# One-pass attention ahead of two gated layers: the first two pairs interleaved, casts moved from ScalarE to VectorE, squares issued earlier, two banks instead of one

## The chip, the cores and the metric
One core of one Trainium2 chip runs the whole program. The metric is device time in microseconds (us). Three runs of the kernel before gave 581.31, 584.41 and 585.79 us, median 584.41 us. The execution that the profiler recorded took 581.65 us; its span, from the first to the last recorded instruction, is 579.8 us.

## The reference, cut to what matters
Inputs are `q`, `k`, `v` of shape (2, 12, 448, 64) in fp32 and a scalar `cap`.

```python
scores = cap * np.tanh((q @ k.T / sqrt(64)) / cap)
attn   = softmax(scores)                 # exp, divided by (row sum + 1e-09)
x      = (attn @ v) laid out as (896 tokens, 768 features)
xn     = x / sqrt(mean(x * x) + 1e-06) * rms_g
y      = (silu-gated product of xn @ w_gate and xn @ w_val) @ w_out
out    = prelu(y @ w_in, alpha) @ w_out2
```

The change touches only the first part, from the scores to `xn`, and the weight preparation that runs beside it.

## The kernel before
**Pairs.** The 24 heads are handled as 12 pairs of heads (`NPAIR`), one pair per turn of the main attention loop; "step i" below is turn i. A pair's 2 x 448 x 448 scores are seven 128-row tiles, worked on as four groups: groups 0, 1 and 2 hold two tiles each (128 x 896), group 3 (`TG`) holds one tile with the last 64 keys of both heads. A group's scores are three products (`qk`, L204: high with high parts, low with high, high with low), because each fp32 operand is split into a rounded part `hi` and a rest `lo`. "Score group (i, g)" below is group g of pair i.

**PSUM.** Groups 0 and 1 take turns in two slots of two banks (`ps_s`, tag "s"). Groups 3 and 2 share one further slot (`third()`, tag "x"), one after the other: the second must wait until ScalarE has read the first. One slot `upper()` (tag "o") holds the value product of a pair (`pv`, L231), one slot tag "u" the row sums (`sums`, L245) or a normalisation factor (`under()`).

**A step.** The order is written out by hand; no scheduler moves it, and every engine executes its part strictly in the order of the program text. In step i TensorE (PE) makes the scores of pair i, then the row sums and the value product of pair i-1. ScalarE (ACT) applies tanh to each score group and one exp to the whole pair (`soft`, L213 and L218). VectorE (DVE) copies the value product of pair i-2 out of PSUM (`evac_o`, tile `ee`, L270), takes reciprocals of row sums that come back by DMA (`recip`, L290 to L301), splits the operands of pair i+1 into `hi` and `lo` (`prep`, L187, L188), and copies the row sums out (`evac_u`, L278) and sends them by DMA (L281).

**Every second step.** For even i from 4 on, two finished pairs are normalised (`norm`, L328, L329): PE spreads the reciprocals over 128 partitions (tile `rps`), DVE multiplies. The first of these products of PE goes to slot "u", the second to slot "o", so the second can only start after DVE's copy `ee` has emptied "o". GpSimd (POOL) then squares the normalised pairs (`square`, L308 to L316), and in step 9 PE adds the squares of the first batch up (`rms_sum`, tile `ms`, L350), which is followed by a square root on ACT in step 9 and a reciprocal on DVE in step 10.

**Weights beside it.** Eight units of packed first-layer weights (`conv[0]` to `conv[7]`, 128 x 768 each) are unpacked meanwhile, one per step: `w_top` (L112, a cast of every fourth bf16 into every second f16, on ACT), `w_bits` (L117, DVE), and for some `w_hi` (L131, a cast, on ACT) and `w_lo` (L136, DVE). POOL forms sums and differences of whole units (`w_sum`, L125; named `sum1` to `sum4`, for two halves g = 0 and 1). The lists `first` and `second` hold these side jobs: `a(i, job)` issues one after the softmax of step i, `z(i, job)` at the end of step i.

Of the kernel before, what the change touches and what calls it, by code (L numbers as in the profile page):

```python
# [7 lines left out]
F32 = mybir.dt.float32  # L8
# [49 lines left out]
def attn_moe_kernel(ctx: ExitStack, tc: tile.TileContext, units, qk_in, v, sel, w, gvec, alpha, cap, out, out_t):  # L58
# [46 lines left out]

    top_of = {}

    def w_top(u):
        n = width(u)
        top_of[u] = tops[n_top[0] % 2][:, :n]  # L110
        n_top[0] += 1
        nc.scalar.copy(top_of[u].bitcast(F16)[:, 1::2], raw_t[u].bitcast(BF16)[:, 4:4 * n + 4:4])  # L112

    def w_bits(u):
        n = width(u)
# [9 lines left out]
        nc.gpsimd.tensor_tensor(out=t, in0=f_t[a], in1=f_t[b], op=op)  # L125
        f_t[out] = t

    def w_hi(u):
        k = width(u) // P if u in units else UK
        h_t[u] = wpool.tile([P, UK, P], F32R, tag="wh", name="wh", bufs=WH)[:, :k]  # L130
        nc.scalar.copy(h_t[u], f_t[u].rearrange("p (k m) -> p k m", m=P))  # L131

    def w_lo(u):
        k = width(u) // P if u in units else UK
# [60 lines left out]
    def third():  # L195
        return ps_x.tile([P, 2, 512], F32, tag="x", name="s")
# [11 lines left out]
    def soft(i):  # L208
        t = pt[i] = sb.tile([P, TILES, S], F32, tag="pt", name="pt")
        done = 0  # L210
        for g in (TG, *range(TG)):
            w = WIDE[g]
            nc.scalar.activation(  # L213
                out=t[:, 2 * g:2 * g + w], in_=st.pop((i, g))[:, :w, :S], func=AF.Tanh, scale=cinv
            )
            if g == TG - 1 or (i == 0 and g == 1):
                to = TILES if g == TG - 1 else 4
                nc.scalar.activation(out=t[:, done:to], in_=t[:, done:to], func=AF.Exp, scale=cap_t)  # L218
                done = to

# [2 lines left out]
    def upper(name):  # L223
        return ps_o.tile([P, 512], F32, tag="o", name=name)

    def pv(i):
        t, vv = pt[i], vt.pop(i)
        oo[i] = upper("oo")
        for c in range(TG + 1):
            for h in range(2):  # L230
                nc.tensor.matmul(  # L231
                    oo[i][h * D:h * D + D, :S], vv[:, 2 * c + h, :], t[:, min(2 * c + h, TILES - 1), :], start=c == 0,
                    stop=c == TG, skip_group_check=True,
                )
        del hi[i], lo[i]

    def tiles_of(i):
        return [pt[i][:, min(n, TILES - 1)] for n in range(TILES + 1)]
# [86 lines left out]
    def norm(i, rps):  # L325
        b, p = divmod(i, NP)
        n, j = group[i]
        nc.tensor.matmul(rps[:, :S], sel_t[:, j, :], r2[n % 2], start=True, stop=True)  # L328
        nc.vector.tensor_tensor(out=xf[b][:, p, :], in0=ee.pop(i), in1=rps[:, :S], op=ALU.mult)  # L329
# [90 lines left out]
    with tc.manual_schedule():  # L420
# [41 lines left out]
        def a(i, fn, *args):  # L462
            first.setdefault(i, []).append((fn, args))

        def z(i, fn, *args):
            second.setdefault(i, []).append((fn, args))
# [5 lines left out]
        for i in range(NPAIR):  # L472
            if i % 2 == 1 and i > 2:
                a(i, recip, (i - 3) // 2)
            a(i, load_raw, i + 2)
            a(i, load_v, i + 1)
            a(i, prep, i + 1)
            if i - 2 in range(len(conv)):
                a(i, w_bits, conv[i - 2])
                if i - 2 < len(conv) - RAW:  # L480
                    a(i, w_next, conv[i - 2])
            if i - 1 in range(len(conv)):
                a(i, w_top, conv[i - 1])
            if i % 2 == 0 and i > 2:
                for j in range(2):
                    z(i, square, i - 4 + j)
        a(9, rms_root, 0)
        for hi_at, lo_at, j in ((3, 4, 0), (4, 5, 1), (9, 10, 6), (11, None, 7)):
            a(hi_at, w_hi, conv[j])
            if lo_at:  # L490
                a(lo_at, w_lo, conv[j])
        for put, n, fn, g in ((z, 6, sum1, 0), (z, 7, sum1, 1), (z, 7, sum2, 0), (a, 8, sum2, 1), (a, 8, sum3, 0),
                              (z, 8, sum3, 1), (z, 10, sum4, 0)):
            put(n, fn, "g", g)
# [3 lines left out]
        for i in range(NPAIR):  # L498
            pairs = i % 2 == 0 and i > 2
            if i > 1:  # L500
                evac_o(i - 2)
            if pairs:
                norm(i - 4, under())
            qk(i, TG, third())
            if pairs:
                norm(i - 3, upper("rps"))
            if i == 9:
                rms_sum(0, upper("ms"))
                rms_keep(0)
                nc.vector.tensor_copy(rstd[0], ms_of[0][:, :S])  # L510
                ms_of[0] = rstd[0]
            for g in range(TG):
                qk(i, g, third() if g == TG - 1 else ps_s.tile([P, 2, 512], F32, tag="s", name="s"))
            soft(i)
            for fn, args in first.pop(i, []):
                fn(*args)
            if i == 1:
                pv(0)
            if i > 0:
                sums(i - 1)  # L520
                evac_u(i - 1)
            if i > 1:
                pv(i - 1)
            if i > 0:
                del pt[i - 1]
            for fn, args in second.pop(i, []):
                fn(*args)
        assert not first and not second
        evac_o(last - 1)
        x = third()  # L530
        for j in range(2):
            norm(last - 3 + j, x[:, j])
        sums_now(last)
        pv(last)
        xnorm(2)
# [633 lines left out]
```

## Time and profile before

| | |
|---|---|
| runs | 581.31, 584.41, 585.79 us |
| profiled execution | 581.65 us, span 579.8 us |
| PE busy | 566.8 us (98% of the span) |
| DVE busy | 393.8 us (68%) |
| ACT busy | 340.1 us (59%) |
| POOL busy | 110.2 us (19%) |
| chain that ended last | PE 87%, DVE 4%, POOL 3%, ACT 2%, issue 2% |

An engine's share over the whole span says little here, since the attention steps fill about the first 112 us and the layers the rest. The places where PE stands still are what the table does not show; they are in the rows further down. Times in the rows are from the start of the span. A row of the timeline that merges several instructions gives the time from the first to the last of them.

### The profile page before, as it was taken

Reading aid. Unit: us, or ns where it says so; the run is one execution under the profiler, and the core shown is the slowest. Engines: PE = TensorE matmul, PEld = TensorE weight load, DVE = VectorE, ACT = ScalarE, POOL = GpSimd, SP = SyncE. Lnnn points to the kernel's source line nnn. Section 1 sums busy time; section 2 is a strip of 40 time slices with the busy share of each in tenths; the row PEclk is TensorE's granted clock in tenths of the full one; section 3 lists DMA queues with packets and bytes.
Section 4 is the critical chain, followed back from the end, with each engine's and each line's share of the span. In section 5 each row is a group of like instructions: output and inputs, shape, how many; then the busy total and the mean of one; then the engine's idle time right before and its main releaser. Section 6 shows DMA issues by size and latency. Waiting matters only on the chain.

```text
span 579.8 us, 7286 instructions
## 1 busy us (share of the span) xinstructions
PE 566.8 (98%) x2891; PEld 469.7 (81%) x2891; DVE 393.8 (68%) x445; ACT 340.1 (59%) x398; POOL 110.2 (19%) x60
## 2 busy tenths in 40 slices
PE   7999988999999999999999999999999999999997
PEld 5544434389899999999999999999999988888996
DVE  5377778799998796769761644979897987522400
ACT  6999979557645644448543443595687877323301
POOL 0022564110044342310000054401451000000000
PEclk9999999999999999999999999999999999999999
DMA  8455511120136335124541653003421335343201
GB/s 274 161 197 181 171 57 44 47 119 1 55 109 218 110 109 167 51 63 155 199 137 46 224 212 110 0 1 118 154 74 37 110 109 181 99 164 126 103 0 64
DMA packets 17946, 66.05 MB, mean 114 GB/s; under 512 B 3704, under 2 KB 4344, under 8 KB 17912
## 3 DMA queue, kind: packets, MB, share of 16 engines
q1 hardware_dynamic: 17336, 65.07, 33.3%
q8 instruction: 23, 0.38, 0.3%
q10 hardware_dynamic: 432, 0.38, 0.2%
q0 software_dynamic: 144, 0.13, 0.1%
q14 instruction: 11, 0.09, 0.0%
HBM read 62.66 MB, written 2.75 MB: 113 GB/s over the span
## 4 chain that ended last, share of the span: by engine, by line
PE 87%; DVE 4%; POOL 3%; ACT 2%; issue 2%; DMA 0%; SPq 0%; POOLq 0%
PE s L401 22%; PE m L401 18%; PE m L690 10%; PE s L714 8%; PE m L714 6%; PE s L690 5%; PE s L740 5%; PE s L204 3%; PE oo L231 3%; PE m L740 2%; POOL wt L125 1%; PE us L245 1%; PE m L414 1%; PE s L414 1%; ACT pt L213 1%
## 5 line engine op out<-in xcount | busy, mean ns | idle before, releaser
L136 DVE TENSOR_TENSOR wl<-wt,wh 128x768 fp32r<-128x768 f32 (+2 forms) x104 | 111.2, 1074 | 79.6 <-ACT wh L131 78.5
L125 POOL TENSOR_TENSOR wt<-wt 128x768 f32<-128x768 f32 x40 | 89.2, 2238 | 262.5 <-DVE wt L117 151.2
L131 ACT CAST wh<-wt 128x768 fp32r<-128x768 f32 (+2 forms) x104 | 82.3, 796 | 90.0 <-PE m L714 24.0
L401 PE MATMUL s<-xx,wh 128*128 128x448 f32 x420 | 100.6, 366 | 0.1
L112 ACT CAST top<-raw 128x768 f16<-128x768 bf16 (+2 forms) x74 | 73.8, 1005 | 41.9 <-DVE wt L117 33.8
L401 PEld LDWEIGHTS s<-xx,wh 128*128 128x128 f32 x420 | 78.7, 188 | 7.7 <-issue 0.9
L117 DVE SCALAR_TENSOR_TENSOR wt<-raw,top 128x768 uint32<-128x768 uint32 (+2 forms) x74 | 72.2, 978 | 0.0
L401 PE MATMUL m<-xx,wh 128*128 128x448 f32 x252 | 60.3, 365 | 0.0
L401 PE MATMUL s<-xx,wl 128*128 128x448 f32 x210 | 54.0, 365 | 0.0
L401 PEld LDWEIGHTS m<-xx,wh 128*128 128x128 f32 x252 | 47.3, 188 | 3.7
L213 ACT ACTIVATE pt<-s,cinv 128x896 f32<-128x896 f32 (+1 forms) x48 | 41.3, 913 | 10.0 <-PE s L204 9.4
L401 PEld LDWEIGHTS s<-xx,wl 128*128 128x128 f32 x210 | 39.4, 188 | 3.1
L231 PE MATMUL oo<-pt,vt 128*64 128x448 f32 x192 | 38.7, 545 | 0.0
L218 ACT ACTIVATE pt<-pt,cap_t 128x3136 f32<-128x3136 f32 (+2 forms) x13 | 35.2, 2711 | 0.4
L231 PEld LDWEIGHTS oo<-pt,vt 128*64 128x64 f32 x192 | 12.8, 136 | 24.8 <-issue 19.0
L401 PE MATMUL m<-xx,wl 128*128 128x448 f32 x126 | 32.3, 365 | 0.0
L690 PE MATMUL m<-b,wh 128*128 128x448 f32 x96 | 27.3, 365 | 0.0
L204 PE MATMUL s<-hi 64*128 64x448 f32 (+1 forms) x84 | 21.5, 440 | 5.0 <-ACT pt L213 4.8
L714 PE MATMUL s<-wh,xx 128*128 128x512 f32 x72 | 25.4, 389 | 0.0
L401 PEld LDWEIGHTS m<-xx,wl 128*128 128x128 f32 x126 | 23.7, 188 | 1.9
L690 PE MATMUL m<-xx,wl 128*128 128x448 f32 x88 | 25.0, 365 | 0.0
L690 PE MATMUL m<-xx,wh 128*128 128x448 f32 x88 | 25.0, 365 | 0.0
(210 smaller groups left out, 1004.3 us busy)
## 6 DMA issues: line engine op xcount, KB each, us to landing
raw<-w_in SPq DMA_DIRECT2D x57, 768.0 KB
raw<-w_in SPq DMA_DIRECT2D x16, 512.0 KB
rw<-qk_in SPq DMA_DIRECT2D x11, 480.0 KB
vt<-v_in SPq DMA_DIRECT2D x12, 256.0 KB
out<-wt SPq DMA_DIRECT2D x7, 256.0 KB
out<-o SPq DMA_DIRECT2D x1, 448.0 KB
gt<-us SPq DMA_DIRECT2D x22, 3.5 KB
rw<-qk_in ACTq DMA_DIRECT2D x1, 256.0 KB
```

Of the source, the lines that this page charges most:

```text
L112: nc.scalar.copy(top_of[u].bitcast(F16)[:, 1::2], raw_t[u].bitcast(BF16)[:, 4:4 * n + 4:4])
L117: nc.vector.scalar_tensor_tensor(out=f_t[u].bitcast(U32), in0=raw_t.pop(u).bitcast(U32)[:, 1:2 * n + 1:2], scalar=13, in1=top_of.pop(u), o ...
L125: nc.gpsimd.tensor_tensor(out=t, in0=f_t[a], in1=f_t[b], op=op)
L131: nc.scalar.copy(h_t[u], f_t[u].rearrange("p (k m) -> p k m", m=P))
L136: nc.vector.tensor_tensor(out=l_t[u], in0=f_t[u].rearrange("p (k m) -> p k m", m=P), in1=h_t[u], op=ALU.subtract)
L204: nc.tensor.matmul(s[:, h, :S], kt[rows, c:c + P], qt[rows, :S], start=m == 0, stop=m == 2, skip_group_check=True,)
L213: nc.scalar.activation(out=t[:, 2 * g:2 * g + w], in_=st.pop((i, g))[:, :w, :S], func=AF.Tanh, scale=cinv)
L231: nc.tensor.matmul(oo[i][h * D:h * D + D, :S], vv[:, 2 * c + h, :], t[:, min(2 * c + h, TILES - 1), :], start=c == 0, stop=c == TG, skip_g ...
L401: nc.tensor.matmul(ps[:, r, :S], lhs, rhs, start=first and n == 0, stop=n == len(mm) - 1, skip_group_check=True,)
L690: nc.tensor.matmul(dst[l], wt[:, o, :], x[l], start=first and wt is wh and x is xh, stop=stop)
L714: nc.tensor.matmul(banks[t // 2][:, t % 2], x[:, c], wt, start=j == 0 and n == 0, stop=j == K2N - 1 and n == 2,)
L740: nc.tensor.matmul(dst[m, l], wt[:, o, :], x[:, l], start=k == 0 and n == 0, stop=k == K2N - 1 and n == 2,)
```

## The change
Five things are edited; what is computed stays the same.

1. **First two pairs.** Step 0 makes its groups in the order 0, 1, 2, 3 instead of 3, 0, 1, 2, and group 3 of pair 0 moves from the slot `third()` to a slot of `ps_s`. The tanh calls of pair 0 follow the same order. In step 1 the value product of pair 0 is cut in two halves, one after score group (1, 0), one after (1, 1), where it stood after all four groups.
2. **Casts to DVE.** `w_top` of the first four units goes from ACT to DVE, to the end of steps 1 to 4. `w_hi` of units 0, 1 and 6 goes from ACT to DVE, to the end of steps 3, 4 and 9, with `w_lo` right behind it (it stood in the steps after).
3. **Squares ahead.** In step 8 the squares of pairs 4 and 5 are issued before two of the weight sums on POOL.
4. **Row sums ahead.** In step 10 the row sums of pair 9 are made before score group (10, 2).
5. **Banks apart.** The last two normalisations after the loop use two different slots; they were halves of one.

```diff
-    def w_top(u):
+    def w_top(u, copy=nc.scalar.copy):
...
-        nc.scalar.copy(top_of[u].bitcast(F16)[:, 1::2], raw_t[u].bitcast(BF16)[:, 4:4 * n + 4:4])
+        copy(top_of[u].bitcast(F16)[:, 1::2], raw_t[u].bitcast(BF16)[:, 4:4 * n + 4:4])
...
-        for g in (TG, *range(TG)):
+        for g in (*range(TG), TG) if i == 0 else (TG, *range(TG)):
...
-    def pv(i):
-        t, vv = pt[i], vt.pop(i)
-        oo[i] = upper("oo")
-        for c in range(TG + 1):
+    def pv(i, cs=range(TG + 1)):
+        t, vv = pt[i], vt[i]
+        if cs[0] == 0:
+            oo[i] = upper("oo")
+        for c in cs:
...
-            if i - 1 in range(len(conv)):
-                a(i, w_top, conv[i - 1])
             if i % 2 == 0 and i > 2:
                 for j in range(2):
-                    z(i, square, i - 4 + j)
+                    (a if i == 8 else z)(i, square, i - 4 + j)
+            if i - 1 in range(len(conv)):
+                if i < 5:
+                    z(i, w_top, conv[i - 1], nc.vector.tensor_copy)
+                else:
+                    a(i, w_top, conv[i - 1])
         a(9, rms_root, 0)
-        for hi_at, lo_at, j in ((3, 4, 0), (4, 5, 1), (9, 10, 6), (11, None, 7)):
-            a(hi_at, w_hi, conv[j])
-            if lo_at:
-                a(lo_at, w_lo, conv[j])
+        for n, j in ((3, 0), (4, 1), (9, 6)):
+            z(n, w_hi, conv[j], nc.vector.tensor_copy)
+            z(n, w_lo, conv[j])
+        a(11, w_hi, conv[7])
...
-            qk(i, TG, third())
+            if i:
+                qk(i, TG, third())
...
-            for g in range(TG):
-                qk(i, g, third() if g == TG - 1 else ps_s.tile([P, 2, 512], F32, tag="s", name="s"))
+            two = lambda: ps_s.tile([P, 2, 512], F32, tag="s", name="s")
+            for g in range(TG - 1):
+                qk(i, g, two())
+                if (i, g) == (1, 0):
+                    pv(0, range(2))
+            if i == 0:
+                qk(0, TG - 1, third())
+                qk(0, TG, two())
+            if i == 1:
+                pv(0, range(2, TG + 1))
+            if i == 10:
+                sums(i - 1)
+            if i:
+                qk(i, TG - 1, third())
...
-        x = third()
-        for j in range(2):
-            norm(last - 3 + j, x[:, j])
+        norm(last - 3, third()[:, 0])
+        norm(last - 2, under())
```

What this makes of the order, at three places. First TensorE in step 1 (`s` a score group, `oo` the value product of pair 0, `us` its row sums); ahead of this piece stand the score groups (1, 3) and (1, 0), and before the change also (1, 1) and (1, 2):

```order
-L231 MATMUL oo<-pt,vt 64x448 x8
+L232 MATMUL oo<-pt,vt 64x448 x4
+L204 MATMUL s<-hi 128x448 x2
+L204 MATMUL s<-hi,lo 128x448 x2
+L204 MATMUL s<-lo,hi 128x448 x2
+L232 MATMUL oo<-pt,vt 64x448 x4
+L204 MATMUL s<-hi 128x448 x2
+L204 MATMUL s<-hi,lo 128x448 x2
+L204 MATMUL s<-lo,hi 128x448 x2
 L245 MATMUL us<-pt,ones 32x448 x6
```

The value product of pair 0 now stands in two halves around score group (1, 1), and score group (1, 2) has gone behind both.

Second, VectorE at the end of step 3 and in step 4 (`us` the copied row sums, `top`, `wh`, `wl` the weight jobs, `ee` the copy that empties slot "o"):

```order
 L117 SCALAR_TENSOR_TENSOR wt<-raw,top_94 128x768
 L278 COPY us<-us 128x448
+L112 CAST top_93<-raw 128x768
+L131 CAST wh<-wt 128x768
+L136 TENSOR_TENSOR wl<-wt,wh 128x768
 L270 COPY ee<-oo 128x448
 L329 TENSOR_TENSOR xf<-ee,rps 128x448 x2
```

Three weight jobs now stand ahead of the copy `ee` of pair 2; in step 9 two of them (`wh`, `wl`) stand in the same way ahead of the copy of pair 8.

Third, GpSimd from step 6 to step 8 (`wt` weight sums, `sq` squares, `s` their running sum, whose number is only a name):

```order
-L316 TENSOR_TENSOR s_473<-s_473,sq 128x448
-L125 TENSOR_TENSOR wt<-wt 128x768 x5
+L316 TENSOR_TENSOR s_470<-s_470,sq 128x448
+L125 TENSOR_TENSOR wt<-wt 128x768 x3
 L312 TENSOR_TENSOR sq<-xf 128x448
-L316 TENSOR_TENSOR s_473<-s_473,sq 128x448
+L316 TENSOR_TENSOR s_470<-s_470,sq 128x448
 L312 TENSOR_TENSOR sq<-xf 128x448
-L125 TENSOR_TENSOR wt<-wt 128x768
+L125 TENSOR_TENSOR wt<-wt 128x768 x3
```

Two weight sums have moved from in front of the squares of pairs 4 and 5 to behind them.

## Rows read from the trace of the kernel before

**Rows 1.** Windows, attention and a later stretch: stretch, length, engines' busy us, PEclk, DMA share, GB/s.

```profile
0.00:116.00 116.00, 106.96 (x673) 53.52 (x674) 78.76 (x117) 95.58 (x86) 35.10 (x27) 0.99 0.43 142
116.00:200.00 84.00, 83.68 (x406) 75.74 (x405) 78.03 (x86) 49.85 (x66) 19.12 (x9) 1.00 0.28 97
```

**Rows 2.** Waits of PE, 0 to 122 us: total us, times, longest us.

```profile
PE s L204 <- ACT pt L213: 4.8, 2, 2.9
PE ms L350 <- POOL s L316: 1.7, 1, 1.7
...
PE s L328 <- DVE xf L329: 0.9, 1, 0.9
PE rps L328 <- DVE us L278: 0.4, 1, 0.4
```

**Rows 3.** Windows of one us around PE's first long wait; columns as in rows 1.

```profile
13.00:14.00 1.00, 1.00 (x3) 0.72 (x3) 0.00 (x0) 1.00 (x1) 0.00 (x0) 0.50 1.02 424
...
17.00:18.00 1.00, 1.00 (x8) 0.34 (x6) 0.00 (x0) 1.00 (x2) 0.00 (x0) 1.00 0.58 224
```

**Rows 4.** Timeline of PE, steps 1 to 3: start us, us, what, idle before.

```profile
12.93 0.70 PE L204 MATMUL s<-hi 128*128 128x448 f32 x1 [2.93 <-ACT pt L213]
...
17.30 3.23 PE L231 MATMUL oo<-pt,vt 128*64 128x448 f32 x16
20.45 1.32 PE L245 MATMUL us<-pt,ones 128*32 128x448 f32 x10
...
22.09 0.47 PE L204 MATMUL s<-hi 128*128 128x448 f32 x1
...
29.74 0.47 PE L204 MATMUL s<-hi 128*128 128x448 f32 x1
```

**Rows 5.** ACT: first tanh in the timeline.

```profile
6.62 0.63 ACT L213 ACTIVATE pt<-s,cinv 128x448 f32<-128x448 f32 x1 [0.24 <-PE s L204]
```

**Rows 6.** Lines of ACT by shape, 0 to 112 us: count, busy us, mean ns, idle before.

```profile
L213 ACT ACTIVATE pt<-s,cinv 128x896 f32<-128x896 f32 x36 | 33.9, 1006 | 7.1 <-PE s L204 6.8
L218 ACT ACTIVATE pt<-pt,cap_t 128x3136 f32<-128x3136 f32 x11 | 32.0, 2913 | 0.4
L112 ACT CAST top<-raw 128x768 f16<-128x768 bf16 x8 | 8.5, 1056 | 0.0
L213 ACT ACTIVATE pt<-s,cinv 128x448 f32<-128x448 f32 x12 | 7.6, 634 | 3.0 <-PE s L204 2.5
L131 ACT CAST wh<-wt 128x768 fp32r<-128x768 f32 x4 | 3.3, 818 | 0.0
L218 ACT ACTIVATE pt<-pt,cap_t 128x1792 f32<-128x1792 f32 x1 | 1.8, 1788 | 0.0
```

**Rows 7.** Timeline of DVE, steps 3 to 5.

```profile
32.03 0.24 DVE L290 SCALAR_TENSOR_TENSOR gf<-gt,eps_t 64x28 f32<-64x28 f32 x1 [1.55 <-DMA gt<-us]
...
32.97 0.65 DVE L187 CAST hi<-rw 128x960 fp32r<-128x960 f32 x1
33.65 1.16 DVE L188 TENSOR_TENSOR lo<-rw,hi 128x960 fp32r<-128x960 f32 x1
34.73 0.98 DVE L117 SCALAR_TENSOR_TENSOR wt<-raw,top 128x768 uint32<-128x768 uint32 x1
...
37.49 0.62 DVE L270 COPY ee<-oo 128x448 f32<-128x448 f32 x1 [1.25 <-PE oo L231]
...
52.02 0.95 DVE L136 TENSOR_TENSOR wl<-wt,wh 128x768 fp32r<-128x768 f32 x1
```

**Rows 8.** Timeline of POOL, steps 7 to 9.

```profile
68.39 8.57 POOL L125 TENSOR_TENSOR wt<-wt 128x768 f32<-128x768 f32 x4 [5.73 <-DVE wt L117]
...
80.62 1.82 POOL L125 TENSOR_TENSOR wt<-wt 128x768 f32<-128x768 f32 x1
```

**Rows 9.** Timeline of DVE, steps 8 to 10.

```profile
72.59 2.67 DVE L188 TENSOR_TENSOR lo<-rw,hi 128x960 fp32r<-128x960 f32 x1
...
82.31 0.23 DVE L290 SCALAR_TENSOR_TENSOR gf<-gt,eps_t 64x28 f32<-64x28 f32 x1
...
88.60 0.62 DVE L270 COPY ee<-oo 128x448 f32<-128x448 f32 x1 [2.10 <-PE oo L231]
```

More of the change, by code (lines that the diff above doesn't have):

```diff
@@ L126, in w_sum, with w_hi @@
         f_t[out] = t
-    def w_hi(u):
+    def w_hi(u, copy=nc.scalar.copy):
         k = width(u) // P if u in units else UK
         h_t[u] = wpool.tile([P, UK, P], F32R, tag="wh", name="wh", bufs=WH)[:, :k]
-        nc.scalar.copy(h_t[u], f_t[u].rearrange("p (k m) -> p k m", m=P))
+        copy(h_t[u], f_t[u].rearrange("p (k m) -> p k m", m=P))
     def w_lo(u):
@@ L215, in soft @@
             )
-            if g == TG - 1 or (i == 0 and g == 1):
-                to = TILES if g == TG - 1 else 4
+            if (i, g) == (0, 1) or g == (TG if i == 0 else TG - 1):
+                to = 4 if (i, g) == (0, 1) else TILES
                 nc.scalar.activation(out=t[:, done:to], in_=t[:, done:to], func=AF.Exp, scale=cap_t)
@@ L234, in pv @@
                 )
-        del hi[i], lo[i]
     def tiles_of(i):
@@ L516, in attn_moe_kernel @@
                 fn(*args)
-            if i == 1:
-                pv(0)
-            if i > 0:
+            if i and i != 10:
                 sums(i - 1)
+            if i:
                 evac_u(i - 1)
[L522 to L525, printed above, removed]
+                if i > 1:
+                    pv(i - 1)
+                del pt[i - 1], hi[i - 1], lo[i - 1], vt[i - 1]
             for fn, args in second.pop(i, []):
```

## The prediction

> **What bounds the kernel now.** I read the windows first. In the first 116 us PE is busy for 106.96 us and so stands still for about 9.0; in the stretch behind it is busy for 83.68 of 84.00 us [rows 1]. So PE's stream sets the time, the layers after the attention hand any earlier start on to the end, and only what takes one of PE's 9 us away, or adds one, can count. The waits of PE say where they are [rows 2]: 4.8 us for ACT in two waits, the longest 2.9 and so the other 1.9; 1.7 for POOL's squares; 0.9 and 0.4 for DVE. The rest is the start, which the change leaves. ACT's total load is not the point: casts taken from it save nothing unless PE waited for them there.
>
> The sum is made against the profiled execution, 581.65 us. It is 2.8 us below the median of the runs, 584.41, so I subtract the same sum from the median.
>
> **Steps 0 to 4.** Before, PE waits 2.93 us until 12.93, for ACT's tanh of score group (0, 2), because (0, 2) and (1, 3) use one slot and ACT took that group last but one [rows 4]. [...] Step 1's four score groups take 17.30 - 12.93 = 4.37 us. A whole step at the high clock takes 29.74 - 22.09 = 7.65, its value product 20.45 - 17.30 = 3.15 and its row sums 22.09 - 20.45 = 1.64 [rows 4], so four groups take 2.86 there, 0.7 each, and the low clock cost 1.5.
>
> Now ACT starts at 6.6 as before [rows 5] with two tanh of 1.01, the exp of four tiles 1.79 and tanh (0, 2) of 1.01 [rows 6]: 11.45. PE is through with pair 0 at 12.93 - 2.93 = 10.0, so its wait is about 1.5 us. The other wait of this length, 1.9 us [rows 2], leaves the attention's average clock at 0.99 [rows 1], so I take the clock to stay high. Then PE runs (1, 3), (1, 0), half a value product, (1, 1), the other half, (1, 2): 11.45 + 2.86 + 3.15 + about 0.3 for one change more between the kinds of product (estimate) = 17.8; row sums until 19.4; three groups of step 2 until 21.6. There a new wait comes: (2, 2) needs ACT to have read (2, 3), and ACT has the exp of pair 1 ahead: 17.8 + tanh 1.01 + exp 2.91 + tanh 0.63 [rows 6] = 22.4. PE waits 0.8, and ends step 2 at 22.4 + 0.7 + 1.64 + 3.15 = 27.9 instead of 29.74: 1.8 gained, with rounding I take 1.6.
>
> DVE doesn't let all of this through. In step 4 the second normalisation waits for the copy `ee` of pair 2, and before that copy DVE now has `w_top`, `w_hi` and `w_lo`. It had 1.25 us to spare there [rows 7]. `w_lo` is 0.95; `w_hi` is a cast like the one of 960 columns in 0.65, scaled to 768 about 0.55 [rows 7]. `w_top` isn't in the trace on DVE: below it is such a cast, 0.55; above, the job on the same strided words with two inputs, 0.98 [rows 7]. I take 0.55, the same kind of operation. Sum 2.05, so `ee` is ready 0.8 later against the rest of DVE's queue. That queue starts with the reciprocal that waits for the DMA of the row sums [rows 7], which comes 1.6 earlier, as the row sums do. 1.6 - 0.8 = 0.8 would pass. The weight load that goes ahead of this DMA is issued earlier too, so up to 0.4 more can come back (estimate). I take **1.2**; bounds 0.3 (`w_top` at 0.98, nothing from the DMA) and 1.6.
>
> [...]
>
> **Step 6.** 0.4 us of PE waits for DVE's copy of the row sums, behind a `w_lo` of 0.95 [rows 2, 7]. This `w_lo` now runs a step earlier, ahead of a DMA wait. **0.4** gained, bounds 0 and 0.4.
>
> **Steps 8 to 10, the squares.** PE waits 1.7 us for the squares [rows 2], which queue behind four weight sums of 8.57 us [rows 8]. Two of these, some 4 us, go behind the squares, so the wait goes: 1.7. But the sums aren't gone. DVE and POOL hold each other up: `lo` takes 1.16 us alone and 2.67 beside the sums [rows 7, 9], the difference being most of a sum of 8.57/4 = 2.14. Then three sums of about 1.82 each [rows 8] follow the squares and end about when the one of 80.62 ended. So DVE's chain of step 9, which begins at 82.31 with the reciprocal [rows 9], starts where it did while PE is 1.7 earlier. Its spare time ahead of the copy `ee` of pair 8 is 2.10 [rows 9]; the new `w_hi` and `w_lo` take 0.55 + 0.95 of it and leave 0.6. So 1.1 of the 1.7 is given back at the second normalisation of step 10, rounded to 1.0. I take **0.7**; bounds 0 and 1.7.
>
> [...]
>
> **Step 10.** PE waits the other 1.9 us here, for ACT, which does the square root between two table loads. The row sums of pair 9, 1.64 us [rows 4], now fill it. PE also changes once more between kinds of product, some 0.3 (estimate), so I take **1.2**; bounds 0.8 and 1.6. ACT's `w_hi` of 0.82 [rows 6] leaves the same stretch, which makes the slot free earlier but isn't needed.
>
> **After the loop.** The second normalisation waited 0.9 us for DVE to read the first out of the same tile [rows 2]. The other slot is free by then. **0.9**, bounds 0.5 (the reciprocal of the last row sums hangs on DVE, which gains less) and 0.9.
>
> **Off the path.** The casts of steps 1, 2 and 4 lie in DVE's waits for PE or a DMA, and no normalisation follows them at once. Should that cover go, each costs its 0.55 to 0.95. SP's and POOL's DMA queues keep their order.
>
> **Sum:** 1.2 + 0.4 + 0.7 + 1.2 + 0.9 = 4.4. 581.65 - 4.4 = 577.25 for a profiled execution, 584.41 - 4.4 = **580.0** for the median.
>
> **The rivals.**
> *DVE never late*: 1.6 + 0.4 + 1.7 + 1.3 + 0.9 = 5.9, so 578.5. For it: DVE has waits of 1.25, 1.55 and 2.10 us. Against: 1.25 and 2.10 us of room must take 2.05 and 1.5 of new work [rows 7, 9].
> *DVE is the new bound*: 0.3 + 0.4 + 0 + 1.2 + 0.9 = 2.8, so 581.6. For it the 2.67 us. Against: there POOL had four sums in a row, now squares lie between.
> *The clock falls again in the shorter wait*, as it did in the 2.93: 1.5 of the first term is paid as before; gain about 3, so 581.4.
> *Slower: the clock stays low.* In its place, steps 1 and 2, PE now changes work more often and has a new wait. [...] Against: once back at 1.00 the clock held, at a mean of 0.99 over the attention [rows 1, 3]. [...]
> *It does not do what it says*: the squares are already off the path. The wait for them [rows 2] excludes that.
>
> **How the numbers follow.** Forecast 0.48, DVE never late 0.18, DVE the bound 0.17, clock falls again 0.11, clock stays low 0.06. The median of three runs can lie 1.5 us off (the runs span 4.5). Range: from the best case less two, 576.5, to the worst of the likely cases plus two, 583.5; what stays out is the low clock and the tails. One per cent is 5.8 us, about what can be told from no change. Faster by more needs under 578.6: about half of "never late" and a part of the forecast's spread, 0.26. Slower by more needs over 590.3: the low clock, 0.06. Within: 0.68.
>
> **What would show it.** In the profile after: PE's wait near 10 us down to about 1.5 and PEclk at 1.00 behind it; a new wait of PE for tanh of 0.8 in step 2; L112 on DVE at 0.55; no wait of `ms` for POOL, but one of `rps` for DVE at the normalisations of steps 4 and 10, of some 0.5 and 1.0; none of the 1.9 and 0.9. It is wrong if PEclk shows longer stretches at 0.50, if DVE's new jobs take over 1 us, or if PE's gain of the attention is not found again at the end.

## The result and the profile after

| | before | after |
|---|---|---|
| median of the runs | 584.61 us (19 runs, 580.61 to 588.91) | 577.24 us (19 runs, 575.45 to 581.93) |
| profiled execution | 581.65 us, span 579.8 | 576.82 us, span 574.9 |
| busy PE / DVE / ACT / POOL | 566.8 / 393.8 / 340.1 / 110.2 us | 565.7 / 396.4 / 334.2 / 110.1 us |

The recorded ratio of the two sets of runs is 0.9887, 95% interval 0.9858 to 0.9916. The two medians alone differ by 7.4 us (ratio 0.9874), where I forecast 4.4, and 577.24 lies under the 578.6 below which the prediction says "faster by more", with a chance of 0.26; "within" had 0.68. Between the two profiled executions it is 4.8 us, close to the forecast; but the terms of the sum came out otherwise, and errors cancelled. Where the other 2.5 us come from is a second question, answered below as far as the runs allow.

The windows of after, columns as in [rows 1]:

```profile
0.00:116.00 116.00, 110.78 (x692) 54.97 (x693) 85.56 (x132) 92.41 (x84) 35.01 (x27) 0.99 0.46 156
116.00:200.00 84.00, 83.69 (x411) 76.68 (x410) 76.65 (x83) 48.55 (x63) 19.11 (x9) 1.00 0.24 85
```

PE stands still for 5.2 us of the first 116, not 9.0. The waits of PE, 0 to 122 us, as in [rows 2]:

```profile
PE s L204 <- ACT pt L213: 3.5, 2, 2.7
...
PE rps L328 <- DVE ee L270: 0.5, 1, 0.5
PE s L204 <- DVE hi L449: 0.2, 1, 0.2
```

POOL's 1.7, the `xf` wait of 0.9 and the wait of 0.4 for `us` are gone, and of the two long waits for ACT one is left. The new wait for `ee` is the one forecast for step 10, at 0.5 instead of 1.0; the one forecast for step 4 is not there. The timeline of PE in steps 1 and 2, against [rows 4]:

```profile
11.08 0.47 PE L204 MATMUL s<-hi 128*128 128x448 f32 x1 [2.74 <-ACT pt L213]
...
12.68 3.25 PE L232 MATMUL oo<-pt,vt 128*64 128x448 f32 x8
...
16.80 1.72 PE L232 MATMUL oo<-pt,vt 128*64 128x448 f32 x8
...
23.90 0.47 PE L204 MATMUL s<-hi 64*128 64x448 f32 x2 [0.72 <-ACT pt L213]
...
29.52 0.47 PE L204 MATMUL s<-hi 128*128 128x448 f32 x1
```

Here the forecast fails. The wait is 2.74 us, not 1.5; the first half of the value product takes 3.25 us, the second, equally long, 1.72; and step 3 starts at 29.52, only 0.2 earlier. The new wait in step 2 is there as forecast, at 0.72 (forecast 0.8). The windows of after show the reason for the two halves, next to [rows 3]:

```profile
13.00:14.00 1.00, 1.00 (x4) 0.24 (x2) 0.00 (x0) 1.00 (x3) 0.00 (x0) 0.50 1.01 412
...
17.00:18.00 1.00, 1.00 (x8) 0.29 (x5) 0.00 (x0) 0.93 (x1) 0.00 (x0) 1.00 0.19 71
```

PEclk is at 0.50 from 13 to 16, as before the change, and at 1.00 again from 17 to 18. Later places gained more than forecast. PE around step 10 and behind the loop:

```profile
85.91 0.47 PE L328 MATMUL rps<-r,sel_t 128*128 128x448 f32 x1
...
87.50 0.47 PE L328 MATMUL rps<-r,sel_t 128*128 128x448 f32 x1 [0.51 <-DVE ee L270]
...
91.76 3.23 PE L232 MATMUL oo<-pt,vt 128*64 128x448 f32 x16
94.92 0.47 PE L204 MATMUL s<-hi 128*128 128x448 f32 x1
...
102.54 0.47 PE L328 MATMUL s<-r,sel_t 128*128 128x448 f32 x1
102.85 0.36 PE L328 MATMUL rps<-r,sel_t 128*128 128x448 f32 x1
```

Reading the same instruction in both traces gives the gain by place, before minus after. Each is the start in before less the start in after, and the step between two of them is what a stretch gained:

| PE starts | before | after | gained so far | in this stretch | forecast |
|---|---|---|---|---|---|
| step 3 | 29.74 | 29.52 | 0.2 | 0.2 | 1.2 |
| first normalisation, step 6 | 53.56 | 52.84 | 0.7 | 0.5 | 0.4 |
| step 9 behind `ms` | 81.66 | 79.09 | 2.6 | 1.85 | 1.7 |
| second normalisation, step 10 | 89.40 | 87.50 | 1.9 | -0.7 | -1.0 |
| step 11 | 98.63 | 94.92 | 3.7 | 1.8 | 1.2 |
| last row sums, behind the loop | 107.99 | 103.14 | 4.85 | 1.1 | 0.9 |
| end of the span | 579.8 | 574.9 | 4.9 | 0 | 0 |

Behind the attention nothing is gained: from the start of the last product `rps` (L328, at 116.10 and 111.24 us) to the end of the span both traces take 463.7 us. I call this time the **tail**; it will tell the kernels below apart.

### The profile page after: what moved, and what is told of

It is laid out like the page before. It is cut to its first block, busy times and chain, and to the rows that moved or that the text cites. A ratio compares the mean times of both kernels' runs of the same rounds, so it can differ in the third digit from the quotient of the medians.

```text
span 574.9 us, 7281 instructions
## 1 busy us (share of the span) xinstructions
PE 565.7 (98%) x2891; PEld 467.5 (81%) x2891; DVE 396.4 (69%) x452; ACT 334.2 (58%) x391; POOL 110.1 (19%) x60
## 4 chain that ended last, share of the span: by engine, by line
PE 94%; DVE 3%; ACT 2%; DMA 1%; issue 0%; ACTq 0%; DVEq 0%
PE s L401 22%; PE m L401 19%; PE m L703 10%; PE s L727 8%; PE oo L232 6%; PE m L727 6%; PE s L703 5%; PE s L753 5%; PE s L204 5%; PE us L245 3%; PE m L753 2%; PE m L414 1%; PE s L414 1%; DMA cap_t<-cap_in 1%; ACT pt L218 1%; ACT pt L213 1%
## 5 line engine op out<-in xcount | busy, mean ns | idle before, releaser
L125 POOL TENSOR_TENSOR wt<-wt 128x768 f32<-128x768 f32 x40 | 87.8, 2201 | 261.3 <-DVE wt L117 150.9
L131 ACT CAST wh<-wt 128x768 fp32r<-128x768 f32 (+1 forms) x101 | 79.9, 795 | 90.7 <-PE m L727 24.0
L401 PE MATMUL s<-xx,wh 128*128 128x448 f32 x420 | 100.6, 366 | 0.1
L112 ACT CAST top<-raw 128x768 f16<-128x768 bf16 (+2 forms) x70 | 69.6, 1002 | 40.3 <-DVE wt L117 35.7
L401 PEld LDWEIGHTS s<-xx,wh 128*128 128x128 f32 x420 | 78.7, 188 | 7.6 <-issue 0.9
L401 PE MATMUL m<-xx,wh 128*128 128x448 f32 x252 | 60.4, 365 | 0.0
L401 PE MATMUL s<-xx,wl 128*128 128x448 f32 x210 | 54.0, 365 | 0.0
L401 PEld LDWEIGHTS m<-xx,wh 128*128 128x128 f32 x252 | 47.3, 188 | 3.7
L401 PEld LDWEIGHTS s<-xx,wl 128*128 128x128 f32 x210 | 39.4, 188 | 3.1
L232 PE MATMUL oo<-pt,vt 128*64 128x448 f32 x192 | 40.4, 563 | 0.0
L401 PE MATMUL m<-xx,wl 128*128 128x448 f32 x126 | 32.4, 365 | 0.0
L401 PEld LDWEIGHTS m<-xx,wl 128*128 128x128 f32 x126 | 23.7, 188 | 1.9
```

The costliest lines, as they stand in the source:

```text
L232: nc.tensor.matmul(oo[i][h * D:h * D + D, :S], vv[:, 2 * c + h, :], t[:, min(2 * c + h, TILES - 1), :], start=c == 0, stop=c == TG, skip_g ...
L401: nc.tensor.matmul(ps[:, r, :S], lhs, rhs, start=first and n == 0, stop=n == len(mm) - 1, skip_group_check=True,)
```

## The experiments

Experiments 1 to 4 share a chip and 17 runs of the kernel before (median 582.75); experiments 5, 6, 7 and 9 share another (17 runs, 584.58), and experiment 8 and the three kernels of 10 a third (20 runs, 582.07). Before's own median thus moves by 2.5 us from set to set. The ratios are the recorded ones; they are not quotients of the two medians.

**1. After without the first edit.** Pair 0 in the old order, its value product in one piece:

```diff
-        for g in (*range(TG), TG) if i == 0 else (TG, *range(TG)):
+        for g in (TG, *range(TG)):
...
-            if i == 1:
-                pv(0, range(2, TG + 1))
...
+            if i == 1:
+                pv(0)
```

> The changed kernel with edit 1 taken back (steps 0 and 1 in the old order), edits 2 to 5 kept. Theory A (the stages add up as the two traces show them): the start is worth 0.2 us of the 4.9 between the spans, so the span is 575.1 us when PE's clock behaves as in the profiles, and the median is 0.2 above the changed kernel. Theory B (the medians differ by 7.4 us, the profiled spans by only 4.9, and the missing 2.5 lie in the start, which is better in most runs than in the profiled one): median 2 to 3 us above the changed kernel. Either way PE waits 2.9 us for tanh near 10 us again, and step 2 has no wait for tanh.

Median 581.65 us (12 runs, 576.76 to 582.66), ratio to before 0.9945 (0.9912 to 0.9978); the profiled run took 581.83. By the medians, which come from two sets, the first edit would be worth over 4 us, more than either theory had, but the trace says otherwise: at 118 us this kernel is only 0.4 us behind after. Its step 3 starts at 29.80 us, 0.3 after after's 29.52, and 1.6 after the 28.19 of an execution of the same attention in which the clock held (shown under experiment 10); by the traces the first edit is worth 0.3 to 1.6. The rest is lost behind the attention, evenly from 153 to about 398 us, with no wait of PE. Windows of this kernel, PE alone:

```profile
200.00:250.00 50.00, 50.00 (x244) 1.00 0.34 111
400.00:450.00 50.00, 50.00 (x248) 1.00 0.30 98
```

and of after:

```profile
200.00:250.00 50.00, 50.00 (x248) 1.00 0.32 111
250.00:300.00 50.00, 50.00 (x249) 1.00 0.43 147
```

At the same granted clock PE ran 244 products in 50 us, not 248 or 249. From start to start they are 206.7 ns apart, in after 202.7; 1,150 products by 4.0 ns are 4.6 us. The runs stand in two groups with this distance: 576.8 to 577.0 (3 of 12) and 580.2 to 582.7 (9). I call it the **slow pace**; experiments 9 and 10 take it up. The tail shows it in one number: 468.3 us here and in experiment 6, 463.7 in before, after and experiments 3, 7 and 8, and 464.2 in experiments 2, 4 and 5, where PE keeps the slow pace only up to 142 to 144 us.

**2. After without the second edit.** All casts back on ACT:

```diff
-                if i < 5:
-                    z(i, w_top, conv[i - 1], nc.vector.tensor_copy)
-                else:
-                    a(i, w_top, conv[i - 1])
+                a(i, w_top, conv[i - 1])
...
-        for n, j in ((3, 0), (4, 1), (9, 6)):
-            z(n, w_hi, conv[j], nc.vector.tensor_copy)
-            z(n, w_lo, conv[j])
-        a(11, w_hi, conv[7])
+        for hi_at, lo_at, j in ((3, 4, 0), (4, 5, 1), (9, 10, 6), (11, None, 7)):
+            a(hi_at, w_hi, conv[j])
+            if lo_at:
+                a(lo_at, w_lo, conv[j])
```

> The changed kernel with edit 2 taken back (all casts on ACT again). Theory A (the casts on DVE pay at the start and cost in step 10): PE's new wait for tanh in step 2 grows from 0.7 to 1.8 us, since the 1.06 us cast stands ahead of that tanh; PE waits again 0.4 us for DVE in step 6; and the wait of 0.5 us for the copy of pair 8 in step 10 is gone. Sum about 1 us longer, span 575.9. Rival (the casts are off the path everywhere, since ACT has time): span within 0.3 of 574.9 and the wait in step 2 stays at 0.7.

One run, 577.29 us, span 575.5. ACT and PE in step 2:

```profile
22.09 1.04 ACT L112 CAST top<-raw 128x768 f16<-128x768 bf16 x1
```

```profile
23.68 0.47 PE L204 MATMUL s<-hi 64*128 64x448 f32 x2 [1.63 <-ACT pt L213]
```

The wait in step 2 is 1.63 us, where after has 0.72: ACT's `w_top` stands ahead of the tanh that PE waits for, as theory A had it (1.8). The wait for `us` in step 6 is back (0.5), the wait for `ee` in step 10 is gone, and 0.22 us of ACT's wait in step 10 is left. At the last `rps` product (111.31) this kernel is only 0.1 us behind after, but the two do not compare: in after's trace the clock fell near 13 us, here it held. It also held in the trace of after with the cuts (experiment 10), whose attention is the same as after's. Against that one this kernel is 0.2 us behind at the start of step 1, 1.1 at step 3 (29.28 against 28.19) and 1.5 at the last `rps` product (111.31 against 109.84). So the second edit is worth about 1.3 us, 0.9 of them in step 2. That ACT has 5.5 us less to do (334.2, not 339.7) counts where a cast stood ahead of a tanh that PE waits for, and the forecast's wait of 0.8 in step 2 holds only together with the second edit.

**3. Before with the squares ahead.**

```diff
...
                 for j in range(2):
-                    z(i, square, i - 4 + j)
+                    (a if i == 8 else z)(i, square, i - 4 + j)
...
```

> The kernel before with edit 3 alone (squares of pairs 4 and 5 ahead of two weight sums). Theory A: PE's wait for the squares goes, 1.7 to 1.9 us, and all of it reaches the end, since DVE has no new casts in step 9 and its spare 2.1 us cover its later start: span 578.0, no wait for the copy of pair 8. Rival (the weight sums behind the squares hold DVE up by themselves): a wait of 0.5 to 1 us at the second normalisation of step 10, span 578.5 to 579.

One run, 581.30 us, span 579.5, more than either theory had. PE does leave step 9 1.87 us earlier, and 0.27 is left at step 11. It goes in step 10, in this kernel's timeline of PE and one window:

```profile
91.16 0.47 PE L204 MATMUL s<-hi 64*128 64x448 f32 x2 [1.85 <-ACT pt L213]
...
91.97 2.45 PE L245 MATMUL us<-pt,ones 128*32 128x448 f32 x10
...
95.11 3.32 PE L231 MATMUL oo<-pt,vt 128*64 128x448 f32 x16
```

```profile
93.00:94.00 1.00, 1.00 (x8) 0.20 (x4) 0.04 (x1) 0.97 (x2) 0.88 (x1) 0.50 0.00 0
```

The wait for ACT is as long as before the change, but this time PEclk falls to 0.50 behind it, and the row sums take 95.11 - 91.97 = 3.14 us, not 1.64. In the trace of before the clock stayed at 1.00 after the same wait:

```profile
93.02 0.47 PE L204 MATMUL s<-hi 64*128 64x448 f32 x2 [1.84 <-ACT pt L213]
```

```profile
94.00:95.00 1.00, 1.00 (x16) 0.26 (x8) 0.91 (x1) 1.00 (x2) 0.10 (x2) 1.00 0.00 0
```

**4. Before with the fourth and fifth edit.**

```diff
+                if (i, g) == (10, TG - 1):
+                    sums(i - 1)
                 qk(i, g, third() if g == TG - 1 else ps_s.tile([P, 2, 512], F32, tag="s", name="s"))
...
-                sums(i - 1)
+                if i != 10:
+                    sums(i - 1)
...
-        x = third()
-        for j in range(2):
-            norm(last - 3 + j, x[:, j])
+        norm(last - 3, third()[:, 0])
+        norm(last - 2, under())
```

> The kernel before with edits 4 and 5 alone (row sums ahead in step 10, two slots after the loop). Theory A, by the difference of the two traces: 1.8 + 1.1 = 2.9 us less, span 576.9. Theory of the prediction: 1.2 + 0.9 = 2.1, span 577.7. If ACT's cast in step 9, which this kernel keeps, holds the tanh back, PE still waits up to 0.5 us for tanh in step 10.

One run, 579.43 us, span 577.7. In step 10 a wait of 0.21 us is left of 1.84, and 1.6 us are gained there (step 11 starts at 96.95, not 98.63); behind the loop another 1.0. Both terms stand on their own. The span shows only 2.1 of this, since the tail takes 464.2 us, not 463.7; that it equals the 577.7 of the prediction's theory is chance.

**5. Before with the squares and the row sums.** Experiments 3 and 4 without the fifth edit:

```diff
-                    z(i, square, i - 4 + j)
+                    (a if i == 8 else z)(i, square, i - 4 + j)
...
+                if (i, g) == (10, TG - 1):
+                    sums(i - 1)
...
-                sums(i - 1)
+                if i != 10:
+                    sums(i - 1)
```

> Before, with the squares ahead in step 8 and the row sums ahead in step 10. With the squares alone PE reached step 10 1.9 us earlier, waited there 1.85 us for ACT as before, the clock fell to 0.50 behind that wait, the row sums of pair 9 took 3.14 us where they take 1.64, and 0.27 was left at step 11. Theory 1 (the squares are worth their wait, 1.7 to 1.9, and it was the clock behind the other wait that took it back): with that wait filled by the row sums, PEclk stays at 1.00 in step 10 and step 11 starts about 3.4 us earlier than 98.63, at 95.2; span 576.3. Theory 2 (the squares bring nothing, since ACT or DVE have their next work no earlier): step 11 starts as with the row sums alone, 96.95, span 577.7 or more.

One run, 578.53 us, span 576.8. PE in step 10:

```profile
90.98 0.48 PE L204 MATMUL s<-hi 64*128 64x448 f32 x2 [0.21 <-ACT pt L213]
91.80 3.23 PE L231 MATMUL oo<-pt,vt 128*64 128x448 f32 x16
94.96 0.47 PE L204 MATMUL s<-hi 128*128 128x448 f32 x1
```

PEclk is 1.00 in step 10, and step 11 starts 3.67 us earlier than before, within 0.05 of after's 94.92. So the squares are worth what they remove once no other wait stands behind them at which the clock can fall. Of this 0.5 us goes at the slow pace, up to about 143 us, and so the span is 0.5 above what theory 1 gave.

**6. After with tanh (0, 2) ahead of the first exp.** PE waits 2.74 us for tanh (0, 2), and ACT does the exp of four tiles first:

```diff
-            if (i, g) == (0, 1) or g == (TG if i == 0 else TG - 1):
-                to = 4 if (i, g) == (0, 1) else TILES
+            if (i, g) == (0, 2) or g == (TG if i == 0 else TG - 1):
+                to = 4 if (i, g) == (0, 2) else TILES
```

> After, with tanh (0, 2) ahead of the exp of the first four tiles in step 0. In the trace of after, PE waits 2.74 us until 11.08 for that tanh, the clock falls at 12.7, and the first half of the value product of pair 0 takes 3.18 us where the second takes 1.66. Theory 1 (the start gave only 0.2 of 1.2 because the wait was longer than I had worked out and the clock fell behind it): tanh (0, 2) now ends at about 9.3, PE's wait is 1.0, PEclk stays at 1.00, both halves take 1.6 to 1.7, step 3 starts 3.3 us earlier than 29.52, and a good part of it (2 to 3.3) is found at the end: span 571.6 to 573, median 574 to 575. Theory 2 (VectorE's chain bounds steps 3 and 4, as the prediction had it): step 3 starts earlier, but the copy ee of pair 2, which has 0.17 us of room, comes when it did, a wait of rps for DVE of 1 us or more appears in step 4, and the end gains under 1.5. Theory 3 (the clock falls there whatever the wait is): wait 1.0, PEclk 0.50 again near 12 to 16, gain about 1.7.

Median 574.13 us (6 runs, five from 573.5 to 574.5, one 578.38), ratio to before 0.9859 (0.981 to 0.9909). The profiled run is the 578.38, which has the slow pace from 147 to 395 us; up to there it shows PE

```profile
10.06 0.61 PE L204 MATMUL s<-hi 128*128 128x448 f32 x1
...
11.82 1.72 PE L232 MATMUL oo<-pt,vt 128*64 128x448 f32 x8
...
26.96 0.47 PE L204 MATMUL s<-hi 128*128 128x448 f32 x1
```

and DVE

```profile
27.62 0.23 DVE L290 SCALAR_TENSOR_TENSOR gf<-gt,eps_t 64x28 f32<-64x28 f32 x1
...
34.71 0.62 DVE L270 COPY ee<-oo 128x448 f32<-128x448 f32 x1 [0.57 <-PE oo L232]
```

No wait for tanh (0, 2), PEclk at 1.00, step 3 2.56 us earlier than in after's trace (theory 1 had 3.3), and all 2.56 are still there at 84 us. Some 1.3 of these are what the fallen clock cost in that trace: where the clock held, step 3 of after comes at 28.19 (experiment 10), 1.2 behind 26.96. DVE holds nothing back: the reciprocal starts 3.3 us earlier than in after (27.62 against 30.96), and the copy `ee` of step 4 waits for PE. Theory 2 is out, and with it my step that DVE would not let all of the start through.

**7. The same with two cast pairs behind the copies `ee`.**

```diff
-        for n, j in ((3, 0), (4, 1), (9, 6)):
-            z(n, w_hi, conv[j], nc.vector.tensor_copy)
-            z(n, w_lo, conv[j])
+        for put, n, j in ((a, 4, 0), (z, 4, 1), (a, 10, 6)):
+            put(n, w_hi, conv[j], nc.vector.tensor_copy)
+            put(n, w_lo, conv[j])
```

> The kernel with tanh (0, 2) first, and w_hi and w_lo of units 0 and 6 on DVE behind the copies ee of pairs 2 and 8 (issued in steps 4 and 10, not at the end of 3 and 9). If DVE's queue ahead of ee is what holds the second normalisations of steps 4 and 10, the wait of rps for ee (0.51 in after at 87.50) goes and the end is 0.5 to 0.7 earlier than with the tanh alone, more if step 4 had a wait there too. If something else ends those waits (the reciprocals that come by DMA), the times of the two kernels are the same within 0.3.

Median 574.60 us (6 runs, 573.34 to 577.93), ratio 0.9879 (0.9826 to 0.9932): not told apart from experiment 6 by the runs. In the traces the wait for `ee` in step 10 is gone and 0.44 us is gained there (0.5 to 0.7 was expected); in step 4 nothing.

**8. After with the wait filled.** The order of after is kept; PE only works through part of the wait:

```diff
+            if i == 1:
+                warm = ps_r.tile([P, 512], F32, tag="u", name="warm")
+                for _ in range(8):
+                    nc.tensor.matmul(warm[:, :P], ones, ones, start=True, stop=True)
             if i:
                 qk(i, TG, third())
```

> After, with eight small products (128 x 128 ones, result unused) on PE behind pair 0's scores, in the wait for tanh (0, 2); the order is otherwise that of after, and the group (1, 3) starts no earlier, at about 11.1. Theory 1 (the clock falls because PE stood still): the idle part of the wait is under 1.3 us, PEclk stays at 1.00 from 12 to 17, the first half of the value product takes 1.6 us, not 3.18, and step 3 starts 1.0 to 1.5 us before 29.52. Theory 2 (the clock falls there for another reason, the start-up or the load of the memory): PEclk is at 0.50 near 13 to 16 all the same and step 3 starts at 29.4 or later.

One run, 575.25 us, span 573.5. PE (a row counts instructions, of which each of the eight products has two):

```profile
8.36 1.95 PE L510 MATMUL warm<-ones 128*128 128x128 f32 x16
11.24 0.47 PE L204 MATMUL s<-hi 128*128 128x448 f32 x1 [0.93 <-ACT pt L213]
...
12.84 1.72 PE L232 MATMUL oo<-pt,vt 128*64 128x448 f32 x8
...
27.97 0.47 PE L204 MATMUL s<-hi 128*128 128x448 f32 x1
```

Pair 0 ended at 8.36, as in after's trace (11.08 - 2.74 = 8.34), and the group behind the wait starts no earlier (11.24). But PEclk stays at 1.00 from 12 to 17, the first half takes 1.72, step 3 starts 1.55 us earlier, and 1.4 of it is found at the end of the span. So by this trace it was PE's standing still that brought the clock down: 0.93 us of rest left it at 1.00, where 2.74 had led to 0.50. This is one execution, and the clock also held in some executions of after without any filling (see below); but in the traces of after and of experiments 1 and 5, where pair 0 ended between 8.3 and 8.6 us and PE then waited 2.74, 3.48 and 3.50 us, it fell.

**9. and 10. Cuts in the layers.** To see what the slow pace does, one product of each row of a first-layer product in the layers is cut in two of 224 columns. In experiment 9 (on the kernel of experiment 1) it is the first product, with both halves marked as the start of a sum; that kernel does not compute the reference's result and stands for its time alone. In 10 it is the second (`n == 1`):

```diff
...
-                nc.tensor.matmul(
-                    ps[:, r, :S], lhs, rhs, start=first and n == 0, stop=n == len(mm) - 1,
...
+                for c in (slice(0, S // 2), slice(S // 2, S)) if cut and n == 0 else (slice(0, S),):
+                    nc.tensor.matmul(
+                        ps[:, r, c], lhs, rhs[:, c], start=first and n == 0, stop=n == len(mm) - 1,
...
```

> After without the edit of the first two pairs, and in the layers the first product of each row of a first-layer product cut in two of 224 columns, which breaks PE's even sequence of 448-column products. Without the cuts the runs of this kernel lie at 576.8 to 577.0 (3 of 12) or 580.2 to 582.7 (9 of 12), and in the slow one that was traced the products follow one another every 206.7 ns from 153 to 395 us, where after has 202.7. Theory 1 (PE falls into one of two paces where its stream is broken and keeps it until the next break): the runs no longer stand in two groups 4.6 us apart, and the number of products in 50 us (244 slow, 248 or 249 fast) changes within one trace. Theory 2 (the pace belongs to the execution as a whole: memory, placement): again two groups about 4.6 us apart and one pace through the trace. The cuts themselves may cost up to 1 us in all.

12 runs from 577.30 to 580.26, median 578.30 (ratio 0.9898, 0.9864 to 0.9932): the two groups are gone, and the median is 3.4 us lower than without the cuts (in another set) although the kernel does more. The profiled run, the lowest, had the fast pace between 264 and 353 us, where no cut stands; a change of pace was not seen in this trace, though it was in those of experiments 1, 2, 4, 5 and 6.

> Before, with the second product of each row of a first-layer product in the layers cut in two of 224 columns. Theory 1 (part of the 7.4 us between the medians is that before runs more often at the slower pace of the products behind 150 us, and a broken stream does not keep that pace): the runs lie within 4 us of one another where before had 8 to 9, and the median is nearer to the low end of before, 580 to 582.5. Theory 2 (before's spread has another origin): a spread of 8 us and a median near 584 stay.

12 runs from 582.34 to 584.88, median 583.11, ratio to before 1.0012 (0.9987 to 1.0037). The spread is as theory 1 had it; the median is not, since it lies 1.0 above the 582.07 of before without cuts in the same set.

> After, with the same cuts. Theory 1: no runs near 581.5 any more, spread under 4 us, and a median 4.5 to 5.5 us below that of the kernel before with the cuts, as the two profiled executions differ (4.9). Theory 2 (the change itself is worth 7 us): the medians with the cuts differ by 6.5 to 8 us.

9 runs from 576.55 to 579.02, median 578.23, ratio 0.9918 (0.9889 to 0.9947).

> The kernel with tanh (0, 2) first and w_hi, w_lo of units 0 and 6 behind the copies ee, with the same cuts. The tanh and the casts were worth 3.3 us at the end in the traces; if the cuts keep the products off the slow pace, the runs lie 3 to 3.5 us below those of after with the cuts, at 572.5 to 575, with no run near 578; if not, runs near 578 stay, one in four as without the cuts.

This one is experiment 7 with the cuts: 6 runs from 573.83 to 575.50, median 574.87, ratio 0.9859 (0.9817 to 0.9902).

The spread falls to 2.5 us in before and after and 1.7 in the third. The medians with the cuts differ by 4.9 us, as the two profiled executions did, and the third lies another 3.4 below, as the traces promised (last `rps` product at 111.24 in after, 107.88 in experiment 7). The lowest runs do not get lower by the cuts, and before's lowest gets 1.8 us higher; only the far ones are gone. The cuts themselves cost more than the 1 us I had allowed: the tail of the four traces with cuts takes 465.0 to 466.4 us. One more thing came with the trace of after with the cuts. PE:

```profile
8.66 0.74 PE L204 MATMUL s<-hi 128*128 128x448 f32 x1
...
11.43 0.47 PE L204 MATMUL s<-hi 128*128 128x448 f32 x1 [1.54 <-ACT pt L213]
...
13.04 1.72 PE L232 MATMUL oo<-pt,vt 128*64 128x448 f32 x8
...
28.19 0.47 PE L204 MATMUL s<-hi 128*128 128x448 f32 x1
```

In this execution of the same attention the start went as forecast: pair 0 ended at 11.43 - 1.54 = 9.9, the wait was 1.54, PEclk stayed at 1.00, and step 3 came at 28.19, 1.55 us before 29.74. The last `rps` product starts at 109.84, 6.3 us before the 116.10 of before.

## Why the prediction held, step by step

**The total.** That 4.9 stands in the traces for a forecast of 4.4 is in part luck: the start gave 1.0 us less than forecast and the later places together 1.4 more. In the execution where the start went as forecast the gain is 6.3, so in its own case the sum was 1.9 too small, and the rival "DVE never late" (5.9, given 0.18) is nearer to it.

**Steps 0 to 4 (forecast 1.2, traced 0.2 or 1.5).** The step that failed is "PE is through with pair 0 at 12.93 - 2.93 = 10.0, so its wait is about 1.5 us". I carried 10.0 over from one execution of before. In the traced execution of after PE was through at 8.34: its products took 0.47 us there, where the execution with the cuts still had 0.74 at 8.66. ACT's tanh (0, 2) did not move with it (the group behind it starts at 11.08 and 11.43), so the wait was 2.74, and the clock fell as in the rival I gave 0.11, though behind a wait that was hardly shorter than the 2.93. Experiment 8, in its one execution, shows the standing still as the cause, at a cost of 1.5 us (0.93 us of rest, PEclk at 1.00, step 3 at 27.97 for 29.52); the last trace shows the forecast's case. There the sum's other parts held: PE took 6.51 us from (1, 3) to the end of (1, 2) (11.43 to 17.94), for which I had 6.3, and the new wait in step 2 was 0.72 for 0.8. Of the 6.3, 0.3 was my estimate for one change more between the kinds of product; no run shows that term alone, and beyond the 2.86 and 3.15 PE took 0.5 here. The 0.4 that I let the weight load bring back no run shows.

Both are executions of one program order. How often each comes can be told from the mean granted clock, which is on record for every run: the traces in which it did not fall have 1.000, after's trace, with its one fall, 0.997. Of after's 19 runs, five have 0.999 or 1.000 and take 575.45 to 575.77 us; the other 14 have 0.994 to 0.997, and none of them is under 576.5. So the clock fell in about three of four; where in a run it fell is known from the traces alone.

**The path through DVE.** "DVE doesn't let all of this through" was wrong. The jobs took what I had estimated (0.63 + 0.56 + 0.96 = 2.15 us against 2.05), but the transfer of the row sums lands earlier by more than PE does: the reciprocal that waits for it starts 1.1 us earlier in after's trace (30.96 for 32.03), where step 3 comes 0.2 earlier, and 3.2 earlier (28.85) in the trace with the cuts, where step 3 comes 1.55 earlier and nothing waits for DVE in step 4. In after's DVE timeline the copy `ee` waits for PE, not the reverse, against [rows 7]:

```profile
30.96 0.24 DVE L290 SCALAR_TENSOR_TENSOR gf<-gt,eps_t 64x28 f32<-64x28 f32 x1 [0.69 <-DMA gt<-us]
...
35.06 0.63 DVE L112 CAST top<-raw 128x768 f16<-128x768 bf16 x1
35.57 0.56 DVE L131 CAST wh<-wt 128x768 fp32r<-128x768 f32 x1
36.16 0.96 DVE L136 TENSOR_TENSOR wl<-wt,wh 128x768 fp32r<-128x768 f32 x1
37.29 0.62 DVE L270 COPY ee<-oo 128x448 f32<-128x448 f32 x1 [0.17 <-PE oo L232]
```

`w_top` at 0.63 lies at the lower end of my bounds (0.55 to 0.98), 0.07 above the plain cast `w_hi` of as many elements (0.56).

**Step 6 (0.4, traced 0.5)** went as forecast; experiment 2 brings the wait back.

**Squares (0.7, traced 1.85 - 0.67 = 1.2).** The mechanism is as forecast, with its sizes a little off. DVE's chain of step 9, against [rows 9]:

```profile
79.74 1.77 DVE L290 SCALAR_TENSOR_TENSOR gf<-gt,eps_t 64x28 f32<-64x28 f32 x1
...
85.37 0.55 DVE L131 CAST wh<-wt 128x768 fp32r<-128x768 f32 x1
85.95 0.96 DVE L136 TENSOR_TENSOR wl<-wt,wh 128x768 fp32r<-128x768 f32 x1
86.83 0.61 DVE L270 COPY ee<-oo 128x448 f32<-128x448 f32 x1
```

and POOL beside its start, against [rows 8]:

```profile
76.06 5.41 POOL L125 TENSOR_TENSOR wt<-wt 128x768 f32<-128x768 f32 x3
```

The reciprocal of 0.23 us now takes 1.77 and ends at 81.51, with POOL's third sum at 81.47. So the chain indeed starts with the end of the sums, 1.0 us before its old end of 82.54; I had left it where it was. The 2.67 us that the prediction counts for its rival "DVE is the new bound" belong to an instruction with two inputs, the subtraction that makes `lo`, and not to a cast.

**Step 10 (1.2, traced 1.8).** The row sums filled the wait of 1.84 completely. The 0.3 for another change between kinds of product was an estimate that no run shows alone: in after's timeline PE takes 5.89 us from the last product of (10, 1), at 89.03, to step 11, and 5.70 over the same stretch of step 11, which has one change less (96.84 to 102.54). That ACT had lost `w_hi` counted after all: where it stayed, 0.21 to 0.22 us of the wait was left (experiments 2, 4 and 5).

**Behind the loop (0.9, traced 1.1)**: the wait went, and a little of the switch with it.

**The median.** I subtracted the sum of one execution from a median. That holds only if runs of both kernels scatter alike. Before had 8.3 us of scatter in that set, after 6.5, with 16 of 19 runs at 575.5 to 578.7 and 3 above 581, while 10 of before's 19 lie at 584.6 or above. With the cuts, which take the scatter away, the medians differ by 4.9 us, not 7.4. I take the other 2.5 for an unequal share of runs at the slow pace in that set. This is shown for the kernels of experiments 1 and 6, whose slow runs were traced. For before, whose traced run had the fast pace, it is inferred from its 54 runs in the three later sets: the 31 of them with a mean granted clock of 0.996 or 0.997 stand in two groups, 22 at 580.4 to 582.2 us and 9 at 584.9 to 586.4, with none between, which is about the distance of the two paces at the same clock. The recorded ratio without the cuts has the interval 0.9858 to 0.9916, and that with them, 0.9918 / 1.0012 = 0.9906, lies inside it, so the 2.5 is not a proved difference either.

**Still open:** what puts PE at the slow pace, and why after the wait of 1.84 us in step 10 the clock held in before and fell in experiment 3. It may not hold in before every time: 23 of its 54 later runs have a mean granted clock of 0.990 to 0.994, lower than that of any trace of before.

## What to carry to other kernels

A wait of TensorE costs more than its length when the clock falls behind it (here 1.5 us more, behind 2.74); look at the granted clock of the microseconds after a wait, and price each wait with and without that. Before moving work off an engine, look whether the waiting engine can be given work, or be given what it waits for first: here one exchanged pair of instructions on ACT (experiment 6) brought 2.6 us against after's trace, and still 1.2 at step 3 against the trace in which the clock had held. And a cast that costs an engine little of its time can cost the waiting engine nearly all of its length (0.9 of 1.04 us), when it stands ahead of what that engine waits for (experiment 2). And when medians differ by more than the traces do, compare the same instruction in both traces until it is clear where the surplus arises, before giving it to the change.

## What the runs showed of the hardware

- TensorE ran the same stream of 128 x 448 products at two paces, both at a granted clock of 1.00: 202.7 and 206.7 ns from start to start. In experiment 1 the slow one lasted for about 240 us and cost 4.6 us, without any wait in that stretch. The pace changed within the traces of experiments 1, 2, 4, 5 and 6: in 2, 4 and 5 from 206.7 to 202.7 near 142 to 144 us, where the products of L414 end and those of L401 begin; in 1 and 6 from 202.7 to 206.7 behind a wait of 0.26 us near 147 to 149, and back near 396 to 399. The tail was 463.7, 464.2 or 468.3 us accordingly.
- The same wait of 1.84 to 1.85 us in step 10 left the clock at 1.00 in the trace of before and at 0.50 in another (experiment 3). Near 11 to 13 us, waits of 1.5 and 1.54 us left it at 1.00 (experiment 2, after with the cuts). Waits of 2.93 and 2.74 us there led to 0.50 (before, after), and behind waits of 2.81, 3.48 and 3.50 us (experiments 3, 1 and 5) the products took 0.57 to 0.74 us, as at 0.50; with eight small products and 0.93 us of rest it stayed at 1.00 (experiment 8).
- In the first microseconds the clock column reads 1.00 while the products take 0.74 us, as later at 0.50, and 0.47 once they are fast. There the durations, not the column, tell when the products have become fast.
